# Moving work between engines at the start of a two-layer attention and MLP kernel, with smaller weight transfers and a new order per stage

## The chip, the core and the metric

The kernel runs on one core of one Trainium2 chip. The metric is device time in microseconds (us), lower is better. Profiled spans are 1.7 to 2.1 us shorter than the device times of the same execution, so spans are compared only with spans and times only with times.

The engines are called as the profile calls them: PE is TensorE (matrix products), PEld its weight loads, DVE is VectorE, ACT is ScalarE, POOL is GpSimd, SP is SyncE, which issues the DMA transfers here.

## The reference

The kernel computes two layers, each a windowed attention and a token-mixing MLP, both with a layer norm in front and a residual. The same weights serve both layers. All inputs are bfloat16.

```python
B, S, D, F = 1, 2048, 512, 1792        # H = 32 heads, Dh = 16, W = 256

def A(x, wqkv, wo):                    # causal attention within a window of 256
    q, k, v = split(x @ wqkv)          # [32 heads, 2048, 16] each
    s = (q @ k.T) * Dh ** -0.5
    s = where(0 <= i - j < W, s, -1e9)
    return merge(softmax(s) @ v) @ wo

def Bm(x, w1, b1, w2, b2):             # mixes tokens, not channels
    u = gelu(einsum("bsd,sf->bdf", layernorm(x), w1) + b1)
    return einsum("bdf,fs->bds", u, w2) + b2     # transposed back to [S, D]

for layer in range(2):
    x = x + A(layernorm(x), wqkv, wo)
    x = x + Bm(layernorm(x), w1, b1, w2, b2)
```

## The kernel before

The source describes the work as a graph of operations, each with an engine, what it reads and writes, and an estimated cost. A list scheduler in the source then walks a model of the machine, and at each step gives an engine the best ranked of the operations that can start earliest. Its output, one order per engine, is what runs. The rank uses a few "knobs" that may differ per *stage*; a stage is one attention block of 256 queries, 0 to 7 in layer 0 and 8 to 15 in layer 1.

```python
    KNOBS = dict(age=2500.0, follow=("pv",), hold=0, evac=0.0, norm=0.0)
    TUNE = {
        0: dict(hold=1, norm=-150000.0),
        1: dict(age=4500.0, hold=1, evac=150000.0, norm=200000.0),
        # ... stages 2 to 15 cut
    }

    def _rank(self, o, now, ready):
        T = self.knobs
        if o.cls is None:                       # everything but PE work
            p = o.prio if o.prio is not None else o.idx
            if p == -2e5:   p += T["evac"]      # evacuations of PSUM
            elif p == -1e5: p += T["norm"]      # normalisation
            return (0, p, o.idx)
        if o.cls == "sc":   k = 0               # scores first
        elif o.cls == "pv":                     # probabilities x V
            k = 1 if self.last in T["follow"] or now - ready[o.idx] > T["age"] else 3
        else:                                   # "f": fillers, all other matmuls
            k = -1 if T["hold"] and self.last == "f" and o in self.prev.users else 2
        return (k, o.prio, o.idx)
```

So PE always prefers a score product (it feeds ACT's exponentials), then fillers, and takes a PV product only when it follows another or has waited longer than `age`. The source declares PSUM, where PE's products land, as eight banks (`PS`): three pairs for scores ("score banks") and two single banks shared by the PV sums and all fillers. There are five buffers `pt` for exponentials; such a buffer is free again when its PV product has run.

The layer norm of a tile of 128 tokens is a chain over two engines:

```python
        def ln_block(t, twice):
            a, b = (1.0 + EPS, EPS * EPS) if twice else (1.0, EPS)
            ln_stats(t)                         # DVE: bn_stats (L522), bn_aggr (L524)
            op("gpsimd", ... tensor_scalar(rstd, agg_var, a, b, mult, add))   # L533, the variance step
            op("gpsimd", ... tensor_tensor(rstd, rstd, mhalf, op=pow))        # L535
            op("vector", ... tensor_scalar(xh_sb, x_sb, mean, rstd, subtract, mult))  # L537
```

K goes into a block-diagonal buffer `kbd`, masked by a column `par` for even and odd heads; V goes likewise into `vbd`, which has to be zeroed first:

```python
            # K, all but the very first 256 columns:
            op("vector", ... tensor_copy(stg[:, ts.slot, 0:n], bank(ft)[:, 0:n]))   # L623, out of PSUM
            for h in range(2):
                op("gpsimd", ... tensor_scalar(kbd[..., h, :], stg[...], par[:, h:h + 1], 0.0, mult, add))  # L626
            # zeroing of vbd for chunks 1 and 2:
            for i in (1, 2) if layer == 0 else ():
                op("gpsimd", ... memset(vbd[i], 0.0), cost=1900, prio=1e3, after=[g.last_w["rs1"]])  # L913
```

The weights of the MLP arrive in transfers of 256 to 896 KB, one semaphore each.

The softmax here doesn't subtract the row's maximum and nothing guards it: scores larger than these inputs give would overflow.

Of the kernel before, what the change touches and what calls it, by code (L numbers as in the profile page):

```python
# [6 lines left out]
dt = mybir.dt  # L7
# [3 lines left out]
P = 128  # L11
# [24 lines left out]
class Op:  # L36
    __slots__ = ("idx", "eng", "fn", "cost", "lat", "prio", "deps", "users", "ndeps", "tiles", "start", "end",
                 "done", "seq", "dma", "extra", "cfg", "cls", "flex", "lock", "issue", "phase")


class Graph:
# [13 lines left out]
    def op(self, eng, fn, reads=(), writes=(), cost=100.0, lat=None, prio=None, dma=False, after=(), holds=(),  # L55
           cfg=None, cls=None, flex=False, lock=False, issue=400.0, phase=None):
        o = Op()
        o.idx, o.eng, o.fn, o.cost, o.dma = len(self.ops), eng, fn, cost, dma
# [74 lines left out]
    def _release(self, o):  # L133
# [15 lines left out]
    KNOBS = dict(age=2500.0, follow=("pv",), hold=0, evac=0.0, norm=0.0)  # L149
    TUNE = {  # L150
        0: dict(hold=1, norm=-150000.0),
        1: dict(age=4500.0, hold=1, evac=150000.0, norm=200000.0),
        2: dict(age=4500.0, hold=1, evac=150000.0, norm=200000.0),
        3: dict(age=4500.0, evac=150000.0, norm=200000.0),
        4: dict(age=4500.0, hold=1, evac=150000.0, norm=200000.0),
        5: dict(age=4500.0, evac=150000.0, norm=200000.0),
        6: dict(hold=1, evac=150000.0, norm=200000.0),
        7: dict(age=4500.0, follow=('sc', 'pv'), hold=1, evac=150000.0, norm=200000.0),
        8: dict(age=4500.0, hold=1, evac=150000.0),
        9: dict(age=4500.0, hold=1, evac=150000.0, norm=200000.0),  # L160
        10: dict(age=4500.0, evac=150000.0, norm=200000.0),
        11: dict(age=4500.0, hold=1, evac=150000.0, norm=200000.0),
        12: dict(age=4500.0, hold=1, evac=150000.0, norm=200000.0),
        13: dict(age=3500.0, hold=1, evac=150000.0, norm=200000.0),
        14: dict(age=4500.0, hold=1, evac=150000.0, norm=-150000.0),
        15: dict(age=2900.0, hold=1, evac=150000.0),
    }

    def _rank(self, o, now, ready):
        T = self.knobs  # L170
        if o.cls is None:
            p = o.prio if o.prio is not None else o.idx
            if p == -2e5:
                p += T["evac"]
            elif p == -1e5:
                p += T["norm"]
            return (0, p, o.idx)

        if o.cls == "sc":
            k = 0  # L180
        elif o.cls == "pv":
            k = 1 if self.last in T["follow"] or now - ready[o.idx] > T["age"] else 3
        else:
            k = -1 if T["hold"] and self.last == "f" and o in self.prev.users else 2
        return (k, o.prio, o.idx)

    def schedule(self):
        self.cfg = self.last = self.prev = None
        self.knobs = self.KNOBS
# [10 lines left out]
        while left:  # L200
            best = None
            for e in self.ENGS:
                m = INF
                ests = []
                for o in cand[e]:
                    t = max(ready[o.idx], free[e])
                    if o.lock:
                        t = max(t, port)
                    if any(tl.slots is None for tl in o.tiles):
                        t = max(t, self._alloc_time(o))  # L210
                    ests.append(t)
                    if t < m:
                        m = t
# [5 lines left out]
            m, e, o = best  # L219
            cand[e].remove(o)  # L220
# [7 lines left out]
            else:  # L228
                if e == "tensor":
                    self.last, self.prev = o.cls, o  # L230
                    if o.phase is not None:
                        self.knobs = dict(self.KNOBS, **self.TUNE.get(o.phase, {}))
# [137 lines left out]
def bass_interleave_layers__sliding_block__mixer_token_mlp__prompt_kernel(  # L370
# [19 lines left out]
    NPT = 5  # L390
    SPLIT = [True, False]
# [4 lines left out]
    with es:  # L396
# [121 lines left out]
        ZEROS = [("zero", 1), ("zero", 2)]  # L518


        def ln_stats(t):
            op("vector", lambda e: e.bn_stats(stats[:, t, :], x_sb[:, t, :]), reads=[f"x{t}"], writes=[f"st{t}"],  # L522
               cost=dve_cost(512), after=late_stats if t in (2, 3) else ())
            op("vector", lambda e: e.bn_aggr(agg[:, t, :], stats[:, t, :]), reads=[f"st{t}"], writes=[f"ag{t}"],  # L524
               cost=130)

        late_stats = []

        def ln_block(t, twice):
# [3 lines left out]
            op("gpsimd", lambda e: e.tensor_scalar(rstd[:, t, :], agg[:, t, 1:2], a, b, op0=ALU.mult, op1=ALU.add),  # L533
               reads=[f"ag{t}"], writes=[f"rs{t}"], cost=272, prio=-1e5)
            op("gpsimd", lambda e: e.tensor_tensor(rstd[:, t, :], rstd[:, t, :], mhalf[:], op=ALU.pow),  # L535
               reads=[f"rs{t}", "mhalf"], writes=[f"rs{t}"], cost=520, prio=-1e5)
            op("vector", lambda e: e.tensor_scalar(xh_sb[:, t, :], x_sb[:, t, :], agg[:, t, 0:1], rstd[:, t, :],  # L537
# [21 lines left out]
        def mm_group(dst, n, mk, reads, cols=512, step=2, prio=None, holds=(), after=()):  # L559

            prio = fprio() if prio is None else prio
            for k0 in range(0, n, step):
# [8 lines left out]
                op("tensor", f, reads=rd, writes=[dst], cost=mm_cost(k1 - k0, cols), prio=prio, holds=holds, after=after, cfg="f",  # L571
# [3 lines left out]
        def qkv(m, before, split):  # L575
# [3 lines left out]
            def transpose(i, wide):  # L579
                t = 4 * m + i  # L580
                if wide is None:
                    op("sync", lambda e: e.dma_start_transpose(xhT[:, tx.slot, :, i * P:(i + 1) * P], xh_sb[:, t, :]),
                       reads=[f"xh{t}"], writes=[(tx, i)], dma=True, cost=900, issue=1200.0, prio=-1e5)
                    return
# [7 lines left out]
                op("tensor", f_tr, reads=[f"xh{t}", "ident"], writes=[ft], cost=4 * 60, prio=fprio(),  # L592
                   holds=[tx], cfg="f", cls="f")
                op("vector", lambda e: e.tensor_copy(
# [4 lines left out]
            def proj(o, which, a, b, wide):  # L599
                ft, n = filler(wide), b - a  # L600
                ts = Tile(p_stg) if which and not wide else None
                mm_group(ft, 4, lambda c: (
                    bank(ft)[:, 0:n], wqkv[:, c, which * 512 + o * P:which * 512 + (o + 1) * P], xhT[:, tx.slot, c, a:b]),
                    [(tx, i) for i in range(a // P, b // P)] + [(f"w{which}", o)], cols=n, step=2 if n > 256 else 4,
                    holds=([ts] if ts else []) + [tk] if which else [tq])
                if which == 0 and m == 0 and a == 0 and not wide:
                    op("scalar", lambda e: e.activation(qT[:, tq.slot, o, a:b], bank(ft)[:, 0:n], ACTF.Copy), reads=[ft],
                       writes=[(tq, o, k) for k in KEYS(a, b)], cost=act_cost(n), prio=-2e5)
                    return
                if which == 0:  # L610
                    op("vector", lambda e: e.tensor_copy(qT[:, tq.slot, o, a:b], bank(ft)[:, 0:n]), reads=[ft],
                       writes=[(tq, o, k) for k in KEYS(a, b)], cost=dve_cost(n, psum=True), prio=-2e5)
                    return
                if wide:
                    for h in range(2):
                        op("vector", lambda e, h=h: e.tensor_scalar(
                            kbd[:, tk.slot, o, a // 64:b // 64, h, :], bank(ft)[:, 0:n].rearrange("p (s n) -> p s n", n=64),
                            par[:, h:h + 1], 0.0, op0=ALU.mult, op1=ALU.add),
                           reads=[ft, ("par", h)], writes=[(tk, "k", o, h, k) for k in KEYS(a, b)],
                           cost=dve_cost(n, psum=True, ptrs=1), prio=-3e5)  # L620
                    late_stats[:] = [g.ops[-1]]
                    return
                op("vector", lambda e: e.tensor_copy(stg[:, ts.slot, 0:n], bank(ft)[:, 0:n]), reads=[ft], writes=[ts],  # L623
                   cost=dve_cost(n, psum=True), prio=-2e5)
                for h in range(2):
                    op("gpsimd", lambda e, h=h: e.tensor_scalar(  # L626
                        kbd[:, tk.slot, o, a // 64:b // 64, h, :], stg[:, ts.slot, 0:n].rearrange("p (s n) -> p s n", n=64),
                        par[:, h:h + 1], 0.0, op0=ALU.mult, op1=ALU.add),
                       reads=[ts, ("par", h)], writes=[(tk, "k", o, h, k) for k in KEYS(a, b)], cost=pool_cost(n, 1))

            def vproj(sp):
                ft, ts = filler(False), Tile(p_stg)
                for k0 in range(0, 4, 2):
# [12 lines left out]
                    op("tensor", f_v, reads=[(tx, sp)] + [("w2", o) for o in range(4)], writes=[ft], cost=mm_cost(4, 256),  # L646
                       prio=fprio(), holds=[ts, tk], cfg="pv", cls="f")
                op("vector", lambda e: e.tensor_copy(  # L648
# [3 lines left out]
                if m:  # L652

                    for h in range(2):
                        op("sync", lambda e, h=h: e.dma_start(
# [6 lines left out]
                for h in range(2):  # L662
                    op("gpsimd", lambda e, h=h: e.tensor_scalar(
# [5 lines left out]
            for a, b in ((0, 256), (256, 512)) if split else ((0, 512),):  # L669
                first = m == 0 and a == 0  # L670
                for i in range(a // P, b // P):
                    before(4 * m + i, first)
                for i in range(a // P, b // P):
                    transpose(i, first if m == 0 else None)
                proj(0, 1, a, b, first)
                proj(0, 0, a, b, first)
# [3 lines left out]
                for o in range(1, 4):  # L680
                    proj(o, 1, a, b, False)
                    proj(o, 0, a, b, False)
# [7 lines left out]
        def attention(c, tqs, tks):  # L690
# [6 lines left out]
            for o2 in range(0, 4, 2):  # L697
# [5 lines left out]
                for su in order:  # L703
# [21 lines left out]
                    prev_sc[0] = op("tensor", f_sc, reads=rd, writes=[tA, tB], cost=cols / 2.4 + 42,  # L725
                                    prio=len(g.ops), after=[prev_sc[0]] if prev_sc[0] else [], cfg="sc", cls="sc", phase=phase[0])
                    for i, ts in enumerate((tA, tB)):
                        op("scalar", lambda e, ts=ts, tp=tp, i=i, cols=cols: e.activation(  # L728
# [4 lines left out]
                    for c0, nc_, w0 in plan[su[0][0]][1]:  # L733
# [8 lines left out]
                        op("vector", f_mask, reads=keys + LD, writes=keys, cost=dve_cost(4 * n * nc_ * 64, 0.5),  # L742
                           lock=True)
                    for k, o, base in su:
# [21 lines left out]
                        op("tensor", f_pv, reads=keys + rd, writes=[od[o]], cost=plan[k][2] * 128 / 2.4 + 42,  # L766
# [5 lines left out]
                        op("vector", lambda e, t=t, tr=tr, q=q: e.tensor_copy(  # L772
# [4 lines left out]
                        for fn, sc in ((ACTF.Ln, 1.0), (ACTF.Exp, -1.0)):  # L777
                            op("scalar", lambda e, tr=tr, fn=fn, sc=sc: e.activation(  # L778
# [3 lines left out]
                        for q in range(2):  # L782
                            op("gpsimd", lambda e, tr=tr, q=q, o=o2 + q: e.tensor_tensor(  # L783
# [4 lines left out]
        def wo_block(c, to, wide):  # L788
            for i in range(2):
                t = 2 * c + i  # L790
                ft = filler(wide)
                mm_group(ft, 4, lambda o, i=i, ft=ft: (
                    bank(ft), oT[:, to.slot, o, i * P:(i + 1) * P], wo_sb[:, o, :]), [(to, o) for o in range(4)] + ["wo"])
                op("vector", lambda e, t=t, ft=ft: e.tensor_tensor(x_sb[:, t, :], x_sb[:, t, :], bank(ft), op=ALU.add),  # L794
# [179 lines left out]
```

## Time and profile before

Three runs took 499.40, 499.74 and 500.93 us. The first lines below are from the page of the kernel before: the span, the busy time of each engine, and the busy share in tenths over 40 slices of 12.5 us, with PEclk, the clock granted to PE in tenths of full rate.

```profile
span 498.4 us, 22922 instructions
PE 467.9 (94%) x10570; PEld 260.9 (52%) x10582; DVE 371.1 (74%) x747; ACT 339.9 (68%) x406; POOL 164.6 (33%) x288
PE   6858979999999999999989999989999999999997
ACT  1528989999999993531576998978899995340000
PEclk8876999999999999999998999999999999999999
```

PE is at 94% over all, but the first three slices are thin on both engines (ACT 1, 5, 2) and the clock is below full there.

The next lines are windows of the kernel before, cut at the end of the last exponential of attention block 0 (37.1 us) and of block 7 (187.6 us): first ACT, then PE. The columns are window, its length, busy time (instructions), mean granted clock, DMA share and GB/s. The last three lines for PE are the stretches in which the clock record shows half rate.

```profile
0.00:37.10 37.10, 12.16 (x16) 0.84 0.46 119
37.10:187.60 150.50, 143.88 (x169) 0.97 0.26 62
187.60:498.40 310.80, 183.86 (x223) 0.99 0.37 95
```

```profile
0.00:37.10 37.10, 25.25 (x544) 0.84 0.46 119
37.10:187.60 150.50, 142.06 (x4168) 0.97 0.26 62
187.60:498.40 310.80, 300.57 (x5870) 0.99 0.37 95
8.20:15.00 6.80, 6.06 (x60) 0.50 1.07 341
32.10:45.70 13.60, 10.52 (x240) 0.50 0.32 60
260.80:264.20 3.40, 3.40 (x38) 0.50 0.05 10
```

This gives three parts with different limits. In the start-up PE is idle about a third of the time and ACT two thirds. In the rest of layer 0 ACT is busy 143.9 of 150.5 us, so ACT, mainly its exponentials, bounds it. From 187.6 us on PE is busy 300.6 of 310.8 us, so PE bounds it. At half rate PE was busy 6.06 + 10.52 + 3.40 = 20.0 us, work that would have taken about half as long at full rate: of the same matmuls without waits (L555, 128x512), 24 fell in the 2.2 us from 261.0 us at half rate and 44 in the 2.2 us from 264.4 us at full rate.

The largest waits of PE, and one of ACT, in the kernel before (engine, line, what released it, or "issue" where the profile shows no releaser: us in total, times, longest):

```profile
PE PS L555 <- issue: 5.0, 2, 2.9
PE PS L755 <- DVE pt L740: 4.2, 1, 4.2
PE PS L589 <- DVE xh_sb L537: 2.6, 2, 1.7
ACT pt L728 <- PE PS L755: 10.2, 4, 8.7
```

The 4.2 us wait is for a mask on DVE (L740). The timeline of DVE shows what DVE did instead, and the line of PE what followed (columns: start, duration, engine, line, operation, out<-in, shape, count):

```profile
29.34 1.25 DVE L522 BATCH_NORM_STATS2 stats<-x_sb 128x6 f32<-128x512 bf16 x2
30.51 0.30 DVE L524 BATCH_NORM_AGGREGATE agg<-stats 128x2 f32<-128x6 f32 x2
30.73 1.25 DVE L522 BATCH_NORM_STATS2 stats<-x_sb 128x6 f32<-128x512 bf16 x2
...
32.39 0.41 DVE L740 TENSOR_TENSOR pt<-pt,ldm 128x512 bf16<-128x512 bf16 x1
32.85 0.33 PE L755 MATMUL PS<-pt,vbd 128*32 128x128 bf16 x4 [4.24 <-DVE pt L740]
```

These statistics belong to tokens that are needed much later. Twelve of them, 0.66 us each, run between 18.9 and 31.9 us, ahead of masks and evacuations that PE and ACT wait for. PE's clock falls to half at the end of that gap, at 32.1 us.

The 2.6 us for `xh_sb` is at the head. The tile view of the kernel before, 5 to 12 us, gives the duration of the normalising operation as minimum/median/maximum in ns, then the first and last start:

```profile
L537 DVE TENSOR_SCALAR xh_sb<-x_sb,agg,rstd x2: 412/1192/1973, 5.9 to 6.4; 128x512 bf16<-128x512 bf16 x2
```

The second of the two took 1.97 us instead of 0.41, beside a memset on POOL (L913).

### The profile page before, as it was taken

Reading aid. Unit: us, or ns where it says so; the run is one execution under the profiler, and the core shown is the slowest. Engines: PE = TensorE matmul, PEld = TensorE weight load, DVE = VectorE, ACT = ScalarE, POOL = GpSimd, SP = SyncE. Lnnn points to the kernel's source line nnn. Section 1 sums busy time; section 2 is a strip of 40 time slices with the busy share of each in tenths; the row PEclk is TensorE's granted clock in tenths of the full one; section 3 lists DMA queues with packets and bytes.
Section 4 is the critical chain, followed back from the end, with each engine's and each line's share of the span. In section 5 each row is a group of like instructions: output and inputs, shape, how many; then the busy total and the mean of one; then the engine's idle time right before and its main releaser. Section 6 shows DMA issues by size and latency. Waiting matters only on the chain.

```text
span 498.4 us, 22922 instructions
## 1 busy us (share of the span) xinstructions
PE 467.9 (94%) x10570; PEld 260.9 (52%) x10582; DVE 371.1 (74%) x747; ACT 339.9 (68%) x406; POOL 164.6 (33%) x288
## 2 busy tenths in 40 slices
PE   6858979999999999999989999989999999999997
PEld 4645545666565554445555556555655555444443
DVE  5898869988988989858776888878889884632222
ACT  1528989999999993531576998978899995340000
POOL 5793525551221214114532534533163231100000
PEclk8876999999999999999998999999999999999999
DMA  8404281111221129340075014260302128643173
GB/s 250 92 12 86 59 170 25 26 25 48 64 67 46 47 72 267 114 136 1 14 130 97 5 25 117 45 165 13 78 25 56 47 65 238 164 129 117 54 203 92
DMA packets 83583, 43.42 MB, mean 87 GB/s; under 512 B 18976, under 2 KB 83488, under 8 KB 83488
## 3 DMA queue, kind: packets, MB, share of 16 engines
q1 hardware_dynamic: 83488, 41.96, 33.1%
q8 instruction: 83, 1.36, 1.1%
q14 instruction: 12, 0.10, 0.1%
HBM read 33.56 MB, written 2.10 MB: 72 GB/s over the span
## 4 chain that ended last, share of the span: by engine, by line
PE 66%; ACT 21%; DVE 9%; issue 2%; DMA 2%; POOL 0%; POOLq 0%
PE PS L555 23%; ACT pt L728 19%; PE PS L553 14%; PE PS L755 10%; PE PS L866 7%; PE PS L713 6%; PE PS L639 5%; DVE stats L522 2%; ACT rl L778 2%; DVE pt L738 1%; DVE x_sb L794 1%; DMA w1b<-in_B_w_dram 1%; DVE stg L623 1%; DMA xhT<-xh_sb 1%; DVE xh_sb L537 1%
## 5 line engine op out<-in xcount | busy, mean ns | idle before, releaser
L728 ACT ACTIVATE pt<-PS 128x1024 bf16<-128x1024 f32 (+1 forms) x304 | 289.0, 1080 | 42.1 <-PE PS L713 29.2
L755 PE MATMUL PS<-pt,vbd 128*32 128x64 bf16 (+3 forms) x1920 | 85.5, 251 | 7.5 <-DVE pt L740 4.2
L755 PE MATMUL PS<-pt,onesbd 128*32 128x64 bf16 (+3 forms) x1920 | 82.0, 236 | 1.4 <-issue 1.4
L738 DVE TENSOR_TENSOR pt<-pt,ldm 128x512 bf16<-128x512 bf16 (+1 forms) x192 | 75.3, 400 | 9.7 <-ACT pt L728 8.4
L783 POOL TENSOR_TENSOR oT<-rl 128x256 bf16<-128x256 f32 x64 | 48.5, 778 | 97.7 <-ACT rl L778 97.3
L755 PEld LDWEIGHTS PS<-pt,vbd 128*32 128x32 bf16 x1920 | 64.2, 139 | 22.5 <-DVE pt L740 4.5
L555 PE MATMUL PS<-xh_sb,w1b 128*32 128x512 bf16 x1040 | 64.6, 381 | 0.6 <-DVE x_sb L794 0.5
L555 PE MATMUL PS<-xhT,wqkv 128*32 128x512 bf16 (+1 forms) x1088 | 62.7, 362 | 1.5 <-DVE stg L648 0.8
L713 PE MATMUL PS<-qT,kbd 32*128 32x64 bf16 (+3 forms) x1920 | 61.5, 234 | 2.8 <-ACT pt L728 2.0
L626 POOL TENSOR_SCALAR kbd<-stg,par 128x512 bf16<-128x512 bf16 (+1 forms) x68 | 50.1, 748 | 39.6 <-DVE stg L623 33.3
L896 DVE SCALAR_TENSOR_TENSOR x_sb<-PS,b2col,x_sb 128x512 bf16<-128x512 f32 x32 | 24.0, 750 | 48.0 <-PE PS L553 38.7
L713 PEld LDWEIGHTS PS<-qT,kbd 32*128 32x128 bf16 x1920 | 27.9, 93 | 51.3 <-ACT pt L728 27.4
L755 PEld LDWEIGHTS PS<-pt,onesbd 128*32 128x32 bf16 x1920 | 51.5, 106 | 3.3 <-issue 1.5
L772 DVE COPY rl<-PS 128x512 f32<-128x512 f32 x64 | 43.8, 685 | 11.6 <-PE PS L755 11.2
L533 POOL TENSOR_SCALAR rstd<-agg 128x1 f32<-128x1 f32 x64 | 13.8, 216 | 115.4 <-DVE agg L524 113.1
L778 ACT ACTIVATE rl<-rl 128x512 f32<-128x512 f32 x64 | 44.7, 702 | 5.6 <-DVE rl L772 5.4
L522 DVE BATCH_NORM_STATS2 stats<-x_sb 128x6 f32<-128x512 bf16 x64 | 43.2, 683 | 0.6
L883 ACT ACTIVATE uT<-rl,b1col 128x512 bf16<-128x512 f32 x28 | 18.0, 711 | 30.5 <-DVE rl L877 30.5
L866 PE MATMUL PS<-xh_sb,w1b 128*128 128x512 bf16 x162 | 36.6, 379 | 1.3 <-DMA w1b<-in_B_w_dram 0.7
L535 POOL TENSOR_TENSOR rstd<-rstd,mhalf 128x1 f32<-128x1 f32 x64 | 36.4, 571 | 4.0
L555 PEld LDWEIGHTS PS<-xhT,wqkv 128*32 128x32 bf16 x1088 | 25.2, 96 | 23.7 <-DVE stg L648 1.7
L555 PEld LDWEIGHTS PS<-xh_sb,w1b 128*32 128x32 bf16 x1040 | 23.7, 96 | 26.4 <-DVE x_sb L794 2.2
(61 smaller groups left out, 538.2 us busy)
## 6 DMA issues: line engine op xcount, KB each, us to landing
w1b<-in_B_w_dram SPq DMA_DIRECT2D x26, 512.0 KB, 4.3
w2b<-in_B_w_dram SPq DMA_DIRECT2D x10, 896.0 KB, 5.3
pt<-in_B_w_dram SPq DMA_DIRECT2D x12, 448.0 KB, 6.5
vbd<-stg SPq DMA_DIRECT2D x48, 64.0 KB, 2.3
out_dram<-x_sb SPq DMA_DIRECT2D x16, 128.0 KB, 1.7
x_sb<-in_A_x_dram SPq DMA_DIRECT2D x3, 512.0 KB, 7.6
wqkv<-in_A_wqkv_dram SPq DMA_DIRECT2D x4, 256.0 KB, 5.6
w1b<-in_B_w_dram SPq DMA_DIRECT2D x4, 256.0 KB, 2.8
```

The costliest lines, as they stand in the source:

```text
L522: op("vector", lambda e: e.bn_stats(stats[:, t, :], x_sb[:, t, :]), reads=[f"x{t}"], writes=[f"st{t}"], cost=dve_cost(512), after=late_sta ...
L553: return e.matmul(o, lhsT=w, rhs=x, start=start, stop=stop, skip_group_check=True)
L555: last = e.matmul(o[j:j + 32], lhsT=w[:, j:j + 32], rhs=x, start=start, stop=stop, tile_position=(0, j), skip_group_check=True)
L626: op("gpsimd", lambda e, h=h: e.tensor_scalar(kbd[:, tk.slot, o, a // 64:b // 64, h, :], stg[:, ts.slot, 0:n].rearrange("p (s n) -> p s n" ...
L713: last = e.matmul(PS[:, 2 * tt[r // 2].slot + r % 2, base + c0 * 64:base + (c0 + n) * 64], lhsT=kbd[32 * r:32 * r + 32, tk.slot, o, jj].re ...
L728: op("scalar", lambda e, ts=ts, tp=tp, i=i, cols=cols: e.activation(pt[:, tp.slot, 2 * i:2 * i + 2, 0:cols], PS[:, 2 * ts.slot:2 * ts.slot ...
L738: return e.tensor_tensor(v, v, msk.unsqueeze(1).to_broadcast([P, 4, w]), op=ALU.mult)
L755: last = e.matmul(bank(t)[32 * r:32 * r + 32, den * 256 + q0 * 64:den * 256 + (q0 + n) * 64], lhsT=onesbd[:] if den else vbd[:, tk.slot, j ...
L772: op("vector", lambda e, t=t, tr=tr, q=q: e.tensor_copy(rl[:, tr.slot, :, q, :], bank(t).rearrange("p (a b) -> p a b", a=2)), reads=[t], w ...
L778: op("scalar", lambda e, tr=tr, fn=fn, sc=sc: e.activation(rl[:, tr.slot, 1], rl[:, tr.slot, 1], fn, scale=sc), reads=[(tr, 0), (tr, 1), " ...
L783: op("gpsimd", lambda e, tr=tr, q=q, o=o2 + q: e.tensor_tensor(oT[:, to.slot, o, :], rl[:, tr.slot, 0, q, :], rl[:, tr.slot, 1, q, :], op= ...
L866: last = e.matmul(PS[:, 2 * tu.slot + tt, :], lhsT=v()[:, sc - b0, k0 + tt * P:k0 + (tt + 1) * P], rhs=xh_sb[:, sc, :], start=(sc == b0), ...
```

## The change

The intent is to start attention sooner and to keep both PE and ACT fed after that. Five things change the operations, and one changes the order of all.

```diff
+        for i in (1, 2):                       # zeroing of vbd: ACT (L538) instead of POOL
+            op("scalar", lambda e, i=i: e.activation(vbd[i], ident_broadcast, ACTF.Copy, scale=0.0), ...)
-            for i in (1, 2) if layer == 0 else ():
-                op("gpsimd", lambda e, i=i: e.memset(vbd[i], 0.0), ...)

-            op("gpsimd", lambda e: e.tensor_scalar(rstd, var, a, b, op0=ALU.mult, op1=ALU.add), cost=272)
+            op("vector:var", lambda e: e.tensor_scalar(rstd, var, a, b, op0=ALU.mult, op1=ALU.add), cost=100)

+                if m == 0:                     # K of the first chunk: ACT (L645), straight out of PSUM
+                    for h in range(2):
+                        op("scalar:evka", lambda e, h=h: e.activation(kbd[..., h, :], at(), ACTF.Copy,
+                            scale=par[:, h:h + 1]), ...)
+                    return
                 op("vector:evk", lambda e: e.tensor_copy(stg[...], at()), ...)     # other chunks as before

+            def kq(o, a, b, wide):             # K and Q of the first chunk share a pair of score banks
+                mode = 2 if wide else KQ[layer] if m == 0 else 0       # KQ = [2, 2]
+                ft = filler(mode == 2) if mode else None
+                ...

-            op("sync", lambda e: e.dma_start(v(), w1v[:, s0:s1, f0:f0 + nf]), writes=[tw], ...)
+            for s in range(0, s1 - s0, n):     # w1, and w2 likewise, in 128 KB pieces, a semaphore wait for each
+                op("sync:w1", lambda e, s=s: e.dma_start(v()[:, s:s + n], w1v[...]), writes=[(tw, s // n)], ...)
```

Every operation now has a *kind* (`stat`, `mask`, `evq`, ...), and each stage may shift the priority of a kind (`move`) or let it seem to start later in the model (`wait`):

```diff
     TUNE = {
-        0: dict(hold=1, norm=-150000.0),
+        0: dict(hold=1, wait=dict(evka=600, pv=600, prod=100), move=dict(stat=150000, rstd=600000,
+             evq=300000, fv=-300, mask=-50000)),
...                                            # stages 1 to 15, and 16 and 17 for the last up-projections
     def _rank(self, o, now, ready):
+        p = (o.idx if o.prio is None else o.prio) + self.move.get(o.kind, 0.0)
...
     # in schedule(), for each candidate:
+                    t += self.wait.get(o.kind, 0.0)
```

The number of transfers that SP issues rises from 154 to 326, and PE changes between its kinds of matmul 408 times instead of 388.

## The prediction

> **What bounds the kernel now.** By the busy times in windows:
> - 0 to 36 us, start-up: PE 24.2 us busy, ACT 9.8 of the last 23. In the timeline DVE runs twelve BATCH_NORM_STATS2 of 0.66 us (18.9 to 31.9 us) for tokens needed later, while PE waits 4.24 us for a mask (wait list) and ACT 8.7 us. The granted clock is then 0.50 from 32 to 44 us.
> - 36 to 188 us, attention of layer 0: ACT is busy 145.4 of 152 us, an exponential taking 1.09 us. ACT bounds it, PE (94 to 97%) close behind.
> - 188 to 498 us: PE 97%, so PE bounds it. Its idle time is single stalls labelled "issue" (2.1 us at 257, 1.4 at 328; also 2.9 at 65, all under full DMA) and 0.7 us for w1b at 432.
>
> **What the change does.**
> 1. Late statistics go behind masks and evacuations in stage 0: 7.9 us of DVE work leaves the start-up. This should remove the 4.2 us PE wait and most of the clock loss (12 us at half rate, estimate 4 to 6 us).
> 2. Zeroing of vbd moves from POOL (two MEMSETs of 1.88 us) to ACT, idle there. The second xh took 1.97 us beside a memset, against a median of 0.41. [...] Gain 1.5 us, if the weights have landed.
> 3. First chunk's K: a DVE copy (0.42 us) and two POOL operations (0.5 each) become two ACT operations (estimate 0.4 each), and K and Q leave the two filler banks. ACT gets 14 of these less 3 Q copies in layer 0, about +4.5 us, a true cost where ACT bounds; about +2 in layer 1.
> 4. Variance on DVE: 64 operations of about 0.15 us; POOL loses 13.8 us. Off the path.
> 5. 128 KB transfers: 154 issues become 326. Worth 0.7 us at 432. The bytes stay, so the "issue" stalls move rather than go.
> 6. New order: PE's switches between score, PV and other matmuls rise from 388 to 408[...].
>
> **Sum.** Start-up: 1.5 + 4.2 + 5 (clock) + 3 (other waits before 36 us), less 4.5 of ACT work: layer 0 ends about 9 us earlier. Its steady state has 6.6 us of ACT idle time, of which the order gets perhaps 2. The rest has 8 to 9 us of PE idle time: perhaps 3[...]. Total 12 to 13 us of 499.7.
>
> **Predicted: 487 us, 8 in 10 between 478 and 495; faster by over 2% 0.64, within 2% 0.32, slower 0.04.**
>
> **What would show it.** 1: no PE wait over 2 us between 14 and 36 us, clock 1.0 from 16 to 44 us. 2: both xh near 0.4 us, the first QKV matmul at 8 us instead of 9.55. 3: ACT over 80% busy from 13 to 36 us, the last exponential of layer 0 at 179 instead of 188 us. 4: POOL near 130 us busy, DVE near 375. 5: no wait for w1b near the end.
>
> **What would make it wrong.** PE or DVE as the real limit of layer 0, so that the earlier start is given back before 188 us; [...] many small issues on SP delaying transposes; or an order better than I credit (then below 480).

One term of the sum: the estimate of 2 us for the 20 more changes between kinds of matmul. The total of 12 to 13 us contains it: 9 for the start-up, 2 for the rest of layer 0, and 3 less that 2 for what follows. The 0.4 us for an ACT operation of step 3 is an estimate from the Q copies that ACT did in the kernel before (L607, 0.39 us for 256 columns); the K operations of that shape took 0.48 us in the changed kernel (L645).

## The result and the profile after

On the same chip, four runs of the kernel before gave a median of 500.13 us (499.40 to 500.93) and four of the changed kernel 479.27 us (478.93 to 479.68). The ratio is 0.9583, with a 95% interval of 0.9565 to 0.9601. Ratios here are the mean time of one kernel's fast runs over that of the other's of the same rounds, so they are not quite the ratio of the medians quoted. All outputs are right.

The page of the changed kernel, in the lines shown of before:

```profile
span 477.1 us, 23213 instructions
PE 458.1 (96%) x10606; PEld 256.6 (54%) x10606; DVE 367.3 (77%) x807; ACT 354.7 (74%) x422; POOL 135.4 (28%) x202
PE   7789998999999999999999999999999999999996
ACT  9789999999999972805489998989999995430000
PEclk9999999999999999999999999999999999999999
```

Its windows, cut at the same two events, now 24.6 and 174.8 us: ACT, then PE, with the columns of before.

```profile
0.00:24.60 24.60, 20.76 (x22) 1.00 0.66 173
24.60:174.80 150.20, 146.87 (x176) 1.00 0.28 66
174.80:477.10 302.30, 187.12 (x225) 1.00 0.36 97
```

```profile
0.00:24.60 24.60, 18.29 (x452) 1.00 0.66 173
24.60:174.80 150.20, 142.39 (x4280) 1.00 0.28 66
174.80:477.10 302.30, 297.46 (x5886) 1.00 0.36 97
```

Of the 21.3 us of span, 12.5 were gained before the end of block 0, 0.3 in the rest of layer 0's attention (150.5 against 150.2), and 8.5 after it (310.8 against 302.3). Counted by kind, PE's idle time between matmuls fell by 11.6 us (25.2 to 13.6) and its busy time by 9.8. The second number is in large part the clock: the work is the same but for some forty small matmul instructions, half of the 20.0 us at half rate is 10.0, and the changed kernel has no half-rate stretch until the very end. That 10.0 and 9.8 agree so well is partly luck, since 10.0 is an upper estimate.

The largest waits of PE in the changed kernel that answer to those of before (the line for `xh_sb` is from the same view of the window 0 to 60 us), and ACT's wait for PV:

```profile
PE PS L752 <- ACT pt L767: 2.3, 6, 0.6
PE PS L578 <- DVE qT L631: 1.7, 3, 0.9
PE PS L678 <- issue: 1.5, 1, 1.5
PE PS L612 <- DVE xh_sb L560: 0.6, 1, 0.6
ACT pt L767 <- PE PS L794: 2.2, 3, 1.0
```

The mask wait is gone, the 2.6 us for `xh_sb` has become 0.6, the "issue" stalls have fallen from single ones of 2.9, 2.1 and 1.4 us to 1.5 and 1.0. ACT's 10.2 us for PV has become 2.2. The normalising operation at the head (tile view, 5 to 12 us) is at its plain duration:

```profile
L560 DVE TENSOR_SCALAR xh_sb<-x_sb,agg,rstd x3: 410/410/411, 5.5 to 11.6; 128x512 bf16<-128x512 bf16 x3
```

### The profile page after: what moved, and what is told of

Same layout as the page of the kernel before. It is cut to its first block, busy times and chain, and to the rows that moved or that the text cites. A ratio compares the mean times of both kernels' runs of the same rounds, so it can differ in the third digit from the quotient of the medians.

```text
span 477.1 us, 23213 instructions
## 1 busy us (share of the span) xinstructions
PE 458.1 (96%) x10606; PEld 256.6 (54%) x10606; DVE 367.3 (77%) x807; ACT 354.7 (74%) x422; POOL 135.4 (28%) x202
## 4 chain that ended last, share of the span: by engine, by line
PE 72%; ACT 17%; DVE 8%; DMA 1%; issue 1%; POOL 0%; POOLq 0%
PE PS L578 28%; ACT pt L767 15%; PE PS L576 15%; PE PS L794 11%; PE PS L910 8%; PE PS L752 7%; PE PS L678 4%; ACT rl L817 2%; DVE stats L545 2%; DVE pt L777 1%; DVE rl L811 1%; DMA xhT<-xh_sb 1%; DVE xh_sb L560 1%; DVE stg L687 1%; DVE qT L631 1%
## 5 line engine op out<-in xcount | busy, mean ns | idle before, releaser
L767 ACT ACTIVATE pt<-PS 128x1024 bf16<-128x1024 f32 (+1 forms) x304 | 286.0, 1049 | 21.8 <-PE PS L752 17.9
L794 PE MATMUL PS<-pt,onesbd 128*32 128x64 bf16 (+3 forms) x1920 | 80.8, 233 | 0.0
L777 DVE TENSOR_TENSOR pt<-pt,ldm 128x512 bf16<-128x512 bf16 (+1 forms) x192 | 73.2, 389 | 8.2 <-ACT pt L767 6.6
L578 PE MATMUL PS<-xh_sb,w1b 128*32 128x512 bf16 x1104 | 69.0, 380 | 0.3
L817 ACT ACTIVATE rl<-rl 128x512 f32<-128x512 f32 x64 | 41.8, 667 | 4.6 <-DVE rl L811 4.2
L654 POOL TENSOR_SCALAR kbd<-stg,par 128x512 bf16<-128x512 bf16 x48 | 38.4, 812 | 15.4 <-DVE stg L651 15.1
L578 PEld LDWEIGHTS PS<-xh_sb,w1b 128*32 128x32 bf16 x1104 | 25.6, 96 | 26.2 <-issue 1.5
L928 ACT ACTIVATE uT<-rl,b1col 128x512 bf16<-128x512 f32 x28 | 18.1, 711 | 28.8 <-DVE rl L922 28.8
L578 PEld LDWEIGHTS PS<-xhT,wqkv 128*32 128x32 bf16 x1088 | 25.3, 96 | 23.3 <-DVE qT L631 2.6
L910 PE MATMUL PS<-xh_sb,w1b 128*128 128x512 bf16 x168 | 37.1, 379 | 0.0
L678 PE MATMUL PS<-wqkv,xhT 128*32 128x256 bf16 x1024 | 33.5, 273 | 3.8 <-issue 1.5
```

The lines of the kernel that those rows point to most:

```text
L578: last = e.matmul(o[j:j + 32], lhsT=w[:, j:j + 32], rhs=x, start=start, stop=stop, tile_position=(0, j), skip_group_check=True)
L678: last = e.matmul(bank(ft)[32 * j:32 * j + 32, sc * 256:(sc + 1) * 256], lhsT=xhT[:, tx.slot, c, tok + 32 * (j % 2):tok + 32 * (j % 2) + 3 ...
L767: op("scalar:exp", lambda e, ts=ts, tp=tp, i=i, cols=cols: e.activation(pt[:, tp.slot, 2 * i:2 * i + 2, 0:cols], PS[:, 2 * ts.slot:2 * ts. ...
L777: return e.tensor_tensor(v, v, msk.unsqueeze(1).to_broadcast([P, 4, w]), op=ALU.mult)
L794: last = e.matmul(bank(t)[32 * r:32 * r + 32, den * 256 + q0 * 64:den * 256 + (q0 + n) * 64], lhsT=onesbd[:] if den else vbd[:, tk.slot, j ...
L817: op("scalar:nrm", lambda e, tr=tr, fn=fn, sc=sc: e.activation(rl[:, tr.slot, 1], rl[:, tr.slot, 1], fn, scale=sc), reads=[(tr, 0), (tr, 1 ...
```

## The experiments

Two accounts were tested against each other. The *account by moves*: the moved operations gave the gain; the start-up saves some 12 us and all later work shifts with it. The *account by order*: the new knobs per stage gave it, in the start-up as well as later, and the moves matter little. Where the texts name theories by letter, the numbers beside each letter say what it expects of the run. The first four experiments keep the changed kernel's order and undo one thing at a time, by editing the orders after scheduling; so do big_transfers_first and k_dve_pool, and keep_warm does the same to the kernel before. The others schedule again. The diffs are shortened: helpers are written out in place and the bookkeeping of dependencies is left out. The late statistics are not among the five changed operations: in the changed kernel the knobs set their place.

This table holds the events read from the traces (us from the start of the span; "block" is the end of the last exponential of an attention block, "gelu" of the last one of a layer).

| kernel | first exp | block 0 | block 1 | block 7 | gelu L0 | gelu L1 | span |
|---|---|---|---|---|---|---|---|
| before | 13.7 | 37.1 | 61.1 | 187.6 | 215.1 | 448.7 | 498.4 |
| after | 9.8 | 24.6 | 50.9 | 174.8 | 201.8 | 427.4 | 477.1 |
| zero_on_pool | 14.3 | 27.4 | 54.7 | 178.5 | 205.5 | 430.7 | 480.4 |
| var_on_pool | 11.8 | 28.0 | 55.0 | 178.8 | 205.8 | 431.3 | 481.0 |
| stats_early | 9.8 | 33.6 | 60.4 | 184.3 | 211.4 | 436.5 | 486.2 |
| big_transfers | 9.8 | 24.5 | 51.0 | 175.1 | 202.1 | 428.4 | 482.5 |
| stats_gated | 13.7 | 27.8 | 47.9 | 189.3 | 215.3 | 446.5 | 496.2 |
| old_knobs | 9.8 | 25.3 | 63.1 | 187.9 | 215.3 | 451.9 | 501.6 |
| knobs_to_2 | 9.8 | 25.6 | 52.7 | 183.1 | 210.6 | 445.2 | 495.1 |

### Zeroing back on POOL, the order kept (zero_on_pool)

```diff
         g.schedule()
+        # the two ops that zero vbd move to POOL, behind the second pow, as before
+        for i, o in enumerate(zs):
+            move(o, "gpsimd", AT + i)
+            o.fn = lambda e, i=i: e.memset(vbd[i + 1], 0.0)
```

> The changed kernel with the zeroing of vbd back on POOL as two MEMSETs, placed as before; every other engine keeps its order. Theory A (a start-up delay is paid twice, once as a PE gap and once as granted clock): the second xh takes about 2 us again, the first QKV matmul starts at about 9 us instead of 7.4, the clock falls to half for some 3 to 7 us near 8 us, and the total is 2 to 5 us longer (481 to 484). Theory B (the new order is all that counts, small start-up delays are absorbed): at most 1 us longer, clock unchanged.

It took 482.77 us (ratio to before 0.9647, 0.9595 to 0.9699; the kernel before had 501.20 on that chip), with a span 3.3 us longer than the changed kernel's. The tile view at the head, 5 to 12 us:

```profile
L560 DVE TENSOR_SCALAR xh_sb<-x_sb,agg,rstd x2: 412/2008/3603, 5.5 to 6.0; 128x512 bf16<-128x512 bf16 x2
```

And what PE waited for it over the whole run (us in total, times, longest):

```profile
PE PS L612 <- DVE xh_sb L560: 3.5, 2, 3.1
```

The second `xh_sb` took 3.60 us beside the memsets, and the clock was at half rate from 10.1 to 13.6 us, so the delay was paid as a wait and in clock, as the account by moves had it. POOL's two memsets took 3.55 us together here (from 5.93 us on). So the same operation took 3.60 us here and 1.97 us in the kernel before beside memsets, and 0.41 us in the changed kernel with none. The delay of about 3.7 us at block 7 is carried almost unchanged to the end (3.3). So the zeroing on POOL costs 3.3 us in the changed kernel, about twice the 1.5 that the prediction gave it. The edit hurts more than the kernel before did, though (3.60 us against 1.97 for the same operation), so 3.3 is a price in this order and not a share of the gain.

### Variance step back on POOL, the order kept (var_on_pool)

```diff
         g.schedule()
+        for o in [o for o in g.order["vector"] if o.kind == "var"]:
+            pow_ = [u for u in o.users if u.kind == "rstd"][0]
+            move(o, "gpsimd", g.order["gpsimd"].index(pow_))
```

> The changed kernel with the 64 variance steps back on POOL, each just before its power step; the other engines keep their order. Both theories: within 1 us of the changed kernel (479 to 480.5), POOL about 14 us busier, DVE about 9 us less. More than 2 us would mean that the step is on a critical path after all.

It took 480.65 us (479.02 to 482.78), ratio 0.9593 (0.9525 to 0.9661). Its fastest run equals the changed kernel's. The profiled run was the slowest of the four and had the clock at half rate from 8.2 to 11.6 and from 18.4 to 21.8 us, which goes with its later block 0 (28.0 instead of 24.6). The placement of this step is worth nothing that these runs resolve, and the case is a warning: one profile can differ by 3 us from another of the same kernel, without any change of its work.

### Late statistics early again, the order kept otherwise (stats_early)

```diff
         g.schedule()
+        for i, o in enumerate(st[4:]):          # statistics 5 to 16 right behind the fourth
+            at = g.order["vector"].index(st[3]) + 1 + i
+            move(o, "vector", at)
```

> The changed kernel with the twelve statistics of the later chunks moved forward on DVE, in one block right after the fourth; all other engines keep their order. Theory A: 7 us of DVE work ahead of the masks opens a PE gap of over 3 us between 11 and 20 us, the clock falls to half for 7 to 14 us after it, total 6 to 12 us longer (485 to 491). Theory B: DVE catches up later, total less than 3 us longer.

It took 488.21 us (ratio 0.9754, 0.9700 to 0.9808), and the span is 9.1 us longer than the changed kernel's. PE's largest wait:

```profile
PE PS L612 <- DVE xh_sb L560: 8.3, 2, 7.8
```

One gap of 7.8 us at 13.3 us, for a normalised tile that stood behind the statistics, and half clock from 18.6 to 28.8 us behind it. The delay is 9.0 us at block 0 and 9.1 at the end. The gap is larger than the one in the kernel before (7.8 us against 4.2) and has another releaser, as the edit puts all twelve in one block. Nothing after block 0 takes it back, which is what the account by moves says of a start-up delay, as long as the later order is the changed kernel's.

### Weight transfers large again, the order of all compute kept (big_transfers)

```diff
         g.schedule()
+        for k, os_ in grps.items():             # the 128 KB pieces of one buffer
+            L = os_[-1]
+            L.fn = L.big                        # one transfer at the place of the last piece
+            for o in os_[:-1]: g.order["sync"].remove(o)
```

> The changed kernel with the weights in large transfers again (256 to 896 KB, each issued where its last part was); compute engines keep their order. My forecast: the bytes are the same, so the PE stalls labelled issue stay within 1 us of the changed kernel's 2.5 us, only a wait of about 1 us for weights comes back: 479.5 to 481. Rival: small transfers shorten the stalls labelled issue; then these stalls grow by 3 us or more here, perhaps with a clock drop, total 3 to 8 us longer.

It took 484.02 us (ratio 0.9669, 0.9612 to 0.9725). It lost 1.0 us until the last gelu and 4.4 after it. The "issue" stalls stayed (2.9 us in all against 2.5), as the forecast had it. The loss at the end goes with one wait of PE:

```profile
PE PS L576 <- DMA w2b<-in_B_w_dram: 2.6, 2, 2.2
```

The clock went to half rate from 466.4 to 469.8 us behind that wait. But the edit issues a merged transfer where its *last* piece stood, later than the kernel before would. That is an artefact of the edit, and the next run was made for it.

### Large transfers, the last weights issued sooner (big_transfers_first)

```diff
+            if k[0] == "w2" and k[2] >= 3:      # the w2b buffers only
+                g.order["sync"].insert(g.order["sync"].index(os_[-2]) + 1, L)
```

> As big_transfers, but each large w2b load is issued right after the place of its last but one part, ahead of the store of the output, as in the kernel before. If the 2.2 us wait for w2b near the end was due to the place of the issue: it goes, and the time is 479 to 481. If the size is the cause: it stays, 483 to 485.

It took 483.09 us (482.28 to 487.19), ratio 0.9680 (0.9628 to 0.9732). The wait for `w2b` is gone, so the place of issue was its cause. The expected 479 to 481 us did not come, though. The profiled run was the slowest one. Its first exponential came late, at 11.6 us instead of 9.8, before any large weight transfer, and the granted clock in the second slice of its page (12 to 24 us) reads 7 tenths (9 in that of the changed kernel). In layer 1 it had a 1.1 us wait for a transposed tile at 249.4 us and two "issue" stalls (PE's waits from 62 to 485 us):

```profile
PE PS L794 <- issue: 1.4, 1, 1.4
PE PS L578 <- issue: 1.1, 1, 1.1
```

With pieces of 128 KB and 172 more issues the changed kernel is not slower by anything these runs show. By the medians small pieces are worth about 4 us here, but these come from two chips. In the profile 5.0 us are lost by the last gelu of layer 0, after the late head, and 3.2 later; what the three faster runs (482.28 to 483.24 us) lose no trace shows. Whether the size of the transfers brings the "issue" stalls stays open: big_transfers, with the same sizes, has in layer 1 a single one of 1.0 us, as the changed kernel has.

### Late statistics by a lower priority, in the kernel before (defer_stats)

```diff
-               cost=dve_cost(512), after=late_stats if t in (2, 3) else ())
+               cost=dve_cost(512), after=..., prio=150000 + len(g.ops) if late else None)
```

> The kernel before with one thing alone: the statistics of the later chunks of layer 0 get a low priority on DVE (the scheduler then re-orders what it likes). Theory A: PE gap of 4.2 us and the 13.6 us of half clock after it go, 7 to 11 us shorter (489 to 493). Theory B (the order in the attention stages is what counts): less than 3 us shorter.

This one is void. Every engine's order came out identical to the kernel before, the gap is still there (timeline of PE in defer_stats), and the time is 500.32 against 499.21 us (ratio 1.0004, 0.9964 to 1.0043):

```profile
33.03 0.33 PE L755 MATMUL PS<-pt,vbd 128*32 128x128 bf16 x4 [4.25 <-DVE pt L740]
```

A priority only ranks operations that can start at the same moment of the model. When nothing else is ready at that moment, a statistic goes first however low it ranks. It serves as a reason to compare the orders before a run is spent, and as a null run: a second profile of the program before. Its span is 496.8 us instead of 498.4, and its PE line is:

```profile
PE 465.6 (94%) x10582; PEld 259.4 (52%) x10582; DVE 371.3 (75%) x747; ACT 340.0 (68%) x406; POOL 164.5 (33%) x288
```

Its half-rate stretches are others (9.9 to 13.3, 30.4 to 37.2 and 259.1 to 262.5 us), with 10.2 us of PE work instead of 20.0. So 9.8 us less work at half rate went with 2.3 us less busy time and 1.6 us less span, where plain halving would give 4.9. In this pair half rate thus cost less than half of its busy time (the head of defer_stats may hide some: its clock record starts at 6.5 us, that of before at 4.8). And one profile's clock is not a constant of the kernel.

### Late statistics behind a mask, in the kernel before (stats_gated)

```diff
-               cost=dve_cost(512), after=late_stats if t in (2, 3) else ())
+               cost=dve_cost(512), after=late_stats if t in (2, 3) else
+                   [last_mask[0]] if t >= 4 and layer == 0 and not twice else ())
```

> Made after defer_stats turned out to be the same program as the kernel before on every engine. The kernel before with the statistics of the later chunks of layer 0 made to wait for the last mask built so far; the rest of the order is left to the old scheduler. Step 1 of my prediction: the 4.2 us PE gap goes, the exponentials of the first block end at 31 us or earlier instead of 37, and the total is 7 to 11 us shorter (489 to 493). Rival, from old_knobs: the start is earlier, but chunk 1 under the old order gives it back (ACT idle for over 8 us between 30 and 63 us), total within 3 us of before.

A true dependency did move them. Block 0 ended at 27.8 instead of 37.1 us and block 1 13.2 us early, with none of the other parts of the change. But by block 7 it was 1.7 us *late*, and the kernel took 496.54 us (ratio 0.9930, 0.9888 to 0.9972). ACT's waits from 72 to 150 us show where most of the gain went:

```profile
ACT pt L733 <- PE PS L762: 9.6, 3, 5.3
```

L762 is the PV product. ACT could not write exponentials, because the `pt` buffers were full and PE had not run the PV products that free them. The changed kernel's ACT waited 1.0 us for PV in its whole stretch from block 0 to block 7. This refutes the plain account by moves: a start-up 9 us shorter is given back unless the later order can hold it.

### PE kept busy through the gap, in the kernel before (keep_warm)

```diff
         g.schedule()
+        keep = op("tensor", f_keep, reads=["ident"], cost=100)   # 60 products of ident by ident
+        g.order["tensor"].insert(first_pv, keep)                 # into the bank that the next op overwrites
```

> The kernel before with 60 dummy matmuls of 128 columns put on PE into the 4.2 us gap at 28.6 us, so that PE is busy there and still waits for the same mask; order otherwise untouched. If the clock is a direct cost (10.7 us of matmul work at half rate after the gap): clock 1.0 from 32 to 46 us and about 5 us shorter (494 to 496). If ACT bounds the stage that follows, as my prediction had it: less than 2 us shorter.

The wait for the mask stays; the half rate that began at its end in the kernel before (32.1 us) should go. The inserted products, in the timeline of PE:

```profile
28.23 3.52 PE L952 MATMUL PS<-ident 128*128 128x128 bf16 x60
```

Two windows of PE after them (busy time, granted clock, DMA share, GB/s):

```profile
36.00:40.00 4.00, 1.96 (x60) 1.00 0.49 93
40.00:44.00 4.00, 3.19 (x88) 0.57 0.47 100
```

It took 497.01 us (ratio 0.9934, 0.9901 to 0.9967), 3.3 us faster by the ratio, where about 5 was expected. The clock stayed full to 40.3 us instead of 32.1, then fell for one stretch of 3.4 us, after PE had been busy only 1.96 of 4 us, with waits of about 1.0 us each. So the clock is a cost of its own beside the wait, and part of what full rate gained became waits for DVE, ACT and DMA (0.94, 0.89 and 1.01 us between 36 and 41 us).

### K of the first chunk by DVE and POOL, PE's order kept (k_dve_pool)

```diff
         g.schedule()
+        for a_, b_ in zip(ks[0::2], ks[1::2]):   # each pair of ACT placements
+            cp = op("vector:kcp", ... tensor_copy(kst[:, n % 4, 0:w], src()))
+            ...                                  # a_ and b_ become POOL tensor_scalar out of kst
```

> The changed kernel with K of the first chunk placed by a DVE copy into a staging tile and two POOL operations instead of two ACT operations, K and Q still in the score banks, PE and SP in the same order. If the placement by ScalarE matters: the first block ends 4 us later or more, and the total is 4 us longer or more (483 or more). If it does not: within 1.5 us (478 to 481).

It took 484.04 us (ratio 0.9687, 0.9647 to 0.9727), with a span 3.6 us longer than the changed kernel's. That profile is of its fastest run; by the medians it is 4.8 us slower. The delay was 0.8 us at block 0, where 4 was expected, then 1.9 for the rest of layer 0, and 3.9 at the first block of layer 1. PE's waits show the added hop:

```profile
PE PS L756 <- POOL kbd L1010: 4.9, 4, 1.7
```

So in this order placing K by ACT is worth about 1.9 us per layer, although ACT is the bound of layer 0: PE's wait for the DVE copy and the POOL operations costs more than ACT's extra work. The order was made for ACT; what an order made for the old path would give is not shown.

### The old path of K with the new knobs (k_old_path)

```diff
-    KQ = [2, 2]
+    KQ = [0, 0]
-                if m == 0:
+                if False:                        # K by DVE and POOL; the rest scheduled anew
```

> The changed kernel with K and Q of the first chunk in the filler banks and K through a DVE copy and two POOL operations, new knobs, re-scheduled. If the placement matters: 4 us longer or more, lost before 62 us, with ACT waiting for scores. If it does not: within 2 us. As re-scheduling alone can cost something, this is read beside a control.

It took 514.09 us (ratio 1.0275, 1.0239 to 1.0311), slower than both kernels. Block 0 came even earlier than in the changed kernel, at 23.6 us. Then ACT stood still in blocks 1 and 2 (waits of ACT from 52 to 102 us):

```profile
ACT pt L767 <- PE PS L752: 18.0, 2, 17.3
ACT rl L817 <- DVE rl L811: 9.5, 1, 9.5
```

This run does not tell what the placement of K costs (k_dve_pool does). It tells that knobs found for one set of operations can be worse than the old knobs for another set.

### The new operations with the old knobs (old_knobs)

```diff
-    AGE, FOLLOW, HOLD = 2500.0, 1, 0
-    TUNE = { 0: dict(hold=1, wait=dict(...), move=dict(...)), ... }
+    KNOBS = dict(age=2500.0, follow=("pv",), hold=0, evac=0.0, norm=0.0)
+    TUNE = { 0: dict(hold=1, norm=-150000.0), ... }        # table and rank of the kernel before
```

> The changed kernel's operations (score banks, K on ACT, small transfers, variance on DVE, zeroing on ACT) with the priority rule and the knobs of the kernel before. Theory A: the head (1.5 to 2 us), the first clock drop (about 3 us) and the weight waits are gained, the statistics still pile up: 489 to 496. Theory B: nothing without the new order, 497 or more.

It took 501.50 us (497.74 to 504.97), ratio 1.0021 (0.9950 to 1.0092): nothing is left of the gain. Block 0 ended at 25.3 us, 11.8 early, and block 1 at 63.1, 2.0 late. One wait of ACT between 25 and 64 us accounts for it:

```profile
ACT pt L756 <- PE PS L783: 14.1, 1, 14.1
```

It is the PV product again. All five `pt` buffers were full, and with `age=4500` in that stage the rule lets PE take fillers first; half clock from 36.7 to 50.3 us came on top.

### The new knobs in the first two stages only (knobs_to_2)

```diff
     def _stage(self, phase):
+        if phase >= 2:                           # stages 2 to 17 by the table of the kernel before
+            T = self.OLD.get(phase, {})
+            ...
```

> The changed kernel with its new knobs in stages 0 and 1 alone, and the old rule and knobs from stage 2 on; the order is the same up to about 70 us. If the start-up order is what counts and it is carried along: the second block ends at 50.9 us, layer 0 12 us earlier than before, and the total is 486 to 490, the 8 us of layer 1 being lost. If the old order of the later stages gives the start back: 494 or more.

Its order equals the changed kernel's up to about 53 us on PE and DVE. It took 496.12 us (ratio 0.9925, 0.9876 to 0.9974). It was 8.4 us ahead of the kernel before at block 1, 4.5 at block 7 and 3.3 at the end. The loss is in ACT's waits for PV (5.4 us in 52 to 183 us), and in PE, which at the end of each layer's attention had no filler left while it waited for a normalised tile:

```profile
PE PS L941 <- DVE xh_sb L591: 7.0, 2, 3.5
```

Set side by side (medians; before-medians of the three chips lie between 499.2 and 501.2 us):

| operations | knobs | us |
|---|---|---|
| before | before | 499.7 |
| before, statistics gated | before | 496.5 |
| after | before | 501.5 |
| after | after in stages 0 and 1 | 496.1 |
| after | after | 479.3 |

The new operations with the old knobs are worth nothing, with the new knobs in two stages about 4 us, and the new knobs in the other sixteen stages add about 17. So the gain needs the new order in all stages. That the order would give it without the new operations is not shown: the old operations with all the new knobs were never run, and k_old_path, one step that way, was slower than both kernels. The account by moves holds with one condition: with the new order in place, undoing a part costs at the end about what it costs in the start-up (3.3 for the zeroing, 9.1 for the statistics; for K, 1.9 of its 3.6 come in layer 1), since the later stages then pass a delay through. These prices are not shares of the gain: the parts and the order do not add up as separate sums.

## Why the prediction was right or wrong

The direction and the range were right: 487 us was predicted, with 478 to 495, and 479.3 came. The forecast of the gain, 12 to 13 us, fell short of the 20.9 that came by 8.

**Step 1, statistics: right in mechanism.** No PE wait over 2 us between 14 and 36 us was forecast; the largest is 1.5. A clock of 1.0 from 16 to 44 us was forecast and came. The pile-up costs 9.1 us in stats_early, near the forecast's 4.2 and 5, but partly by luck, as its gap is another one (7.8 us, for a tile). In the kernel before, stats_gated gained 9.3 us at block 0. The means differ from what the prediction assumed, though: stats_gated shows that it also goes by one dependency, and old_knobs that it goes with the old knobs.

**Step 2, zeroing: right, undersized.** Both `xh_sb` operations took 0.41 us as forecast, and the first QKV matmul came at 7.4 us (8 was forecast). Undoing it costs 3.3 us (1.5 was forecast).

**Step 3, K on ACT: the sign was wrong.** The forecast charged 4.5 us of ACT work as a true cost in layer 0. ACT does get busier, by 14.8 us over all: 7.1 are the zeroing, and K takes 9.5 where Q took 3.0, which is the 6.5 that the forecast had for both layers. But k_dve_pool shows that undoing the move costs 3.6 us. The forecast counted only ACT's time, not the latency of the path through DVE and POOL that PE waited for (4.9 us in k_dve_pool). ACT's share of 13 to 36 us was forecast above 80%, and the end of layer 0's exponentials at 179 us; they came at 81% and 174.8. What the score banks alone give was not tested: k_dve_pool keeps K and Q in them.

**Step 4, variance: right.** Its 64 operations on DVE took 0.15 us each (L556). It is off the path; POOL fell to 135.4 us (130 was forecast). DVE was forecast at 375 and fell to 367.3.

**Step 5, transfers: the wait for `w1b` of 0.7 us is gone, as forecast.** "The 'issue' stalls move rather than go" failed: 2.9 + 2.1 + 1.4 us became 1.5 + 1.0. That the bytes decide was the guess, from DMA shares of 1.56, 1.25 and 1.19 during the three stalls; during the two of the changed kernel the share was 1.10 and 0.18. Their cause is not settled.

**The sum, part by part.** The start-up was forecast at 9 us and gave 12.5. The steady part of layer 0 was forecast at 2 and gave 0.3; ACT's idle time did fall from 6.6 to 3.3 us, but its busy time rose by 3.0. The rest was forecast at 1 net (3, less 2) and gave 8.5. This last term is the step that failed most: the forecast took the order to be worth little once PE bounds, and the order was worth far more. knobs_to_2, with the new operations and the old knobs there, took 312.0 us from block 7 to the end, against 310.8 before and 302.3 after. Of the 8.5, idle time of PE gave 5.4 (10.2 to 4.8 us; about 3.5 of either is the tail after the last matmul) and busy time 3.1, of which 1.7 is the clock at 260.8 to 264.2 us and 1.4 is not explained. A cost for the 20 more changes between kinds of matmul was not shown: PE's idle time and its busy time both fell.

**The clock term.** About 5 us were forecast, from 32 to 44 us alone. By halving, the profile of before shows 10.0: 3.0 of them at the head (8.2 to 15.0) and 1.7 in layer 1 had been left out. Both are upper estimates, as defer_stats shows. The profile is also one of those with a low clock: over 21 executions of the kernel before on three chips the mean clock was 0.973 to 0.990 (0.976 in the profile). The eight at 0.985 or more took 498.3 us in the mean, the ten at 0.979 or less 501.6. The changed kernel had 0.996 to 0.999.

**What would make it wrong.** The prediction named an early start given back before 188 us, and an order better than it credited. The second happened. The first is what stats_gated, old_knobs and k_old_path did, so the warning was right, and what kept the changed kernel from it is the order of the later stages.

**What stays open.** The cause of the "issue" stalls; which single knob does what; and differences of 2 us or less, as the kernel before itself ranged from 496.1 to 502.7 us over its runs, and the changed kernel was not run again beside the variants. Tests that schedule the old K path with other knobs could not be built (the scheduler got stuck; no run shows this), so the placement was tested with the order kept. No variant beat the changed kernel.

## What to carry to other kernels

An early start is easy to get and easy to lose: ask which buffer fills up in the stages behind it (here the five `pt`, freed only by PV products that ranked last), and check at the end of every stage whether the lead is still there. To price one part of a change in a scheduled kernel, keep the order and swap the one operation, because the variant that was scheduled anew with the old K path took 35 us more than the changed kernel, of which the path itself is 4. And ask of a gap on PE whether a half-rate stretch follows it: that is a second cost, though here a smaller one than plain halving gives (2.3 us of busy time instead of 4.9 between defer_stats and the kernel before), and it does not follow every gap: in the kernel before, half rate came behind gaps of 4.24 us (28.6 us) and 2.13 us (257.3 us), but not behind one of 2.87 us (64.7 us).
